# Two decode layers with a windowed KV cache: V pages issued from ScalarE's DMA queue instead of SyncE's

## The chip, the cores and the metric

The kernel runs on one core of one Trainium2 chip. The metric is the device time of one execution in microseconds (us). A core has the engines TensorE (PE in the profile, with PEld for its weight loads), VectorE (DVE), ScalarE (ACT), GpSimd (POOL) and SyncE (SP), and 16 DMA engines that move data between HBM and the on-chip memory. Each engine works through its own instructions in order. A DMA is started by an instruction of one of the engines, and stands in that engine's DMA queue; in this kernel these are SP's and ACT's.

## The reference

One token passes through attention and a gated feed-forward network (FFN), twice, with the same weights and caches both times. There are 32 heads of width 192, and each attends to the last 4096 positions of its own K and V cache.

```python
def _A_ref(x, k_cache, v_cache, wq, wo):      # x: (1, 1, 640); caches: (1, 32, 32768, 192), bf16
    W = min(4096, max(256, Sk // 4))          # 4096
    q = (x @ wq).reshape(B, Sq, Hq, Dh).transpose(0, 2, 1, 3)
    k = k_cache[:, :, Sk - W:, :]
    v = v_cache[:, :, Sk - W:, :]
    scores = jnp.einsum("bhqd,bhkd->bhqk", q, k) * (Dh ** -0.5)
    o = jnp.einsum("bhqk,bhkd->bhqd", _softmax(scores), v)
    return o.transpose(0, 2, 1, 3).reshape(B, Sq, Hq * Dh) @ wo

def _B_ref(x, w1, w3, w2):                    # 640 -> 1536 -> 640
    return (_silu(x @ w1) * (x @ w3)) @ w2

for _ in range(2):
    x = x + _A_ref(_layernorm(x), A_k_cache, A_v_cache, A_wq, A_wo)
    x = x + _B_ref(_layernorm(x), B_w1, B_w3, B_w2)
```

## The kernel before

All large data comes into one on-chip buffer, `arena`, of 16 slots of 128 x 6144 bf16 values (1.5 MB each; "page" below). A page is the K or the V window of one head, one fifth of wq, nine of the 48 chunks of wo, or a part of the FFN weights. The list `loads` (lines 147 to 172) fixes an order for all 145 of them. For each layer it holds the five q pages; then, step by step, the V page of head position i - 10 and the K page of position i; then six wo pages and four FFN pages (`fa` to `fd`). Text below numbers the loads 0 to 144 in this order: 0 to 4 are wq, 5 to 14 the first ten K pages, 15 the first V page, and from there V and K alternate. Loads 58 and 124 are the last K pages of the two layers, 68 and 134 the last V pages, 69 to 74 and 135 to 140 the wo pages, 75 to 78 and 141 to 144 the FFN pages. Some wo and FFN pages come in several DMAs.

`refill` (line 174) gives each free slot to the next load of the list and writes the DMA's issue, and `done` (line 186) frees a slot as its page has been used and calls `refill`. So an issue stands in the program just behind the last use of the page that held the slot. The K pages of 13 heads (`RETAIN`) stay in the arena from layer 0 to layer 1. In layer 0 they take slots away one by one, until three are left for all other loads: the last V pages, wo, the FFN, and wq of layer 1. In layer 1 each comes free with its use.

`attention` (line 407) runs over 42 steps. Step i multiplies the probabilities with V page i - 10 (`v_page`) and the query weights with K page i (`k_page`), whose 4-byte transposes on DVE come first (line 262). Eight heads are a block. After the last K page of a block, `softmax_head` takes maxima on DVE, writes one half of a bias on ACT (line 284) and the exponential on ACT (line 289). `build_w` then places the next block's query weights in `wst` (line 249 on ACT, line 251 on POOL), without which its K pages can't be multiplied. Two steps later, `softmax_place` copies the probabilities to `ptm` (line 302; five copies on ACT, three on DVE), without which the block's V pages can't. `combine` copies a finished block's sums on ACT (line 321). After the last step come `wo_proj`, the residual, a layer norm and `ffn`.

The helper `pin` keeps every engine's instructions in the order of the program text. Waits are set by the framework. A DMA waits for the last reader of its slot and for the slot's previous load. The framework also gives each DMA of SP and ACT one of eight completion counters, and a DMA waits until the previous transfer on its counter has landed. The counters are dealt out in the order in which the framework has scheduled the DMAs of both queues; with one queue, that is eight loads back.

Of the kernel before, what the change touches and what calls it, by code (L numbers as in the profile page):

```python
# [40 lines left out]
def kernel(  # L41
# [13 lines left out]
    nc = tc.nc  # L55
# [11 lines left out]
    def pin(ins):  # L67
        tc.keep_in_program_order(ins)
        return ins
# [104 lines left out]
    def refill():  # L174
        while free and loads:
            key, parts = loads.pop(0)
            s = free.pop(0)
            home[key] = s
            for off, n, src in parts:
                dst = arena[:, s * PGW + off:s * PGW + off + n] if off is not None else keep[:]  # L180
                pin(nc.sync.dma_start(out=dst, in_=src))  # L181

    def page(key):
        return arena[:, home[key] * PGW:home[key] * PGW + PGW]
# [1 line left out]
    def done(key):  # L186
        free.append(home.pop(key))
        refill()
# [218 lines left out]
    def attention(layer):  # L407
# [27 lines left out]
        wo_proj(layer)  # L435

    refill()
    ob = cst.tile([P, NCH], BF16, name="ob")
    for layer in range(2):
# [34 lines left out]
```

## Time and profile before

| what | value |
|---|---|
| time, median of 3 runs (lowest to highest) | 542.97 us (542.94 to 543.52) |
| span of the profiled execution, first to last instruction | 546.6 us |
| bytes moved, mean rate over the span | 224.34 MB, 410 GB/s |
| busy time of PE, DVE, ACT, POOL | 288.2, 222.9, 41.9, 13.2 us |
| packets on SP's queue (q1) and on ACT's (q10) | 22608 and 144 |
| rate from 0 to 14 us | 357 GB/s |
| rate from 306 to 318 us and from 318 to 330 us (between the layers) | 355 and 349 GB/s |
| rate from 530 to 541 us (last weights) | 301 GB/s |

The page splits the span into 40 slices and gives each engine's busy share by slice in tenths; the row "DMA" is the mean share of the 16 DMA engines. A row of instructions gives its start or its line, the time, engine, operation, and what it writes from what; brackets at its end hold the idle time of the engine before it and what ended that. In rows of DMA issues, "SPq" or "ACTq" is the queue of the issuing engine, and the last number is the median time from issue to landing. Rows of waits give the total, the count and the longest. A row for a stretch of time gives the busy time of PE, PEld, DVE, ACT and POOL, then PE's granted clock, the DMA share and GB/s. The rates of single stretches in the table are of this last kind.

### The profile page before, as it was taken

How to read it: one execution, taken by the hardware profiler on the slowest of the kernel's cores; microseconds unless marked ns; L12 is line 12 of the kernel's file. 1: busy time of each engine (PE TensorE's matmuls, PEld its weight loads, DVE VectorE, ACT ScalarE, POOL GpSimd, SP SyncE). 2: the span in 40 equal slices, each digit the busy share in tenths (PEclk: the TensorE clock that was granted, in tenths of full speed). 3: DMA queues.
4: the chain of work that ended last, by engine and by line, in shares of the span. 5: the costliest groups of instructions: out<-in, count | busy, mean ns of one | idle time of the engine just before them, and what ended most of it. 6: DMA issues, size and time to landing. Idle time of an engine off the chain costs nothing.

```text
span 546.6 us, 5673 instructions
## 1 busy us (share of the span) xinstructions
PE 288.2 (53%) x2400; PEld 119.9 (22%) x2400; DVE 222.9 (41%) x262; ACT 41.9 (8%) x107; POOL 13.2 (2%) x50
## 2 busy tenths in 40 slices
PE   2355455555564655743544356767465566553544
PEld 1111122222221222211222122333121222221211
DVE  2189755565446654410012057234524744530011
ACT  1100200020001100010001010211001100020000
POOL 5000000000000000000000000000000000000000
PEclk9579595667665776555556558896866766565656
DMA  8999999999999999999999989999999999999993
GB/s 353 430 420 428 421 427 424 424 423 424 426 424 423 424 427 422 423 418 428 417 389 397 370 355 419 424 426 422 425 421 426 423 427 427 423 425 423 420 415 156
DMA packets 22777, 224.34 MB, mean 410 GB/s; under 512 B 2784, under 2 KB 3168, under 8 KB 5472
## 3 DMA queue, kind: packets, MB, share of 16 engines
q1 hardware_dynamic: 22608, 223.98, 98.3%
q8 instruction: 19, 0.31, 0.2%
q14 instruction: 6, 0.05, 0.0%
q10 hardware_dynamic: 144, 0.00, 0.0%
HBM read 223.97 MB, written 0.00 MB: 410 GB/s over the span
## 4 chain that ended last, share of the span: by engine, by line
DMA 79%; PE 11%; DVE 6%; ACT 1%; issue 1%; SPq 1%; POOL 0%; ACTq 0%; DVEq 0%
DMA arena<-in_A_k_cache_dram 54%; DMA arena<-in_A_v_cache_dram 9%; DMA arena<-in_A_wo_dram 7%; PE s_ps L72 7%; DMA arena<-in_B_w_dram 5%; DVE arena L262 4%; DMA arena<-in_A_wq_dram 4%; PE o_ps L72 3%; PE y_ps L72 1%; SPq L181 1%; PE q_ps L72 1%; ACT w L289 0%; DVE t L274 0%; ACT ptm L302 0%; DVE w L292 0%
## 5 line engine op out<-in xcount | busy, mean ns | idle before, releaser
L72 PE MATMUL s_ps<-arena,wst 128*32 128x512 bf16 x768 | 164.0, 523 | 154.5 <-DVE arena L262 149.1
L262 DVE STREAM_TRANSPOSE arena<-arena 128x1536 uint32<-128x1536 uint32 x102 | 174.8, 1753 | 110.7 <-DMA arena<-in_A_k_cache_dram 108.8
L72 PE MATMUL o_ps<-arena,ptm 128*16 128x384 bf16 (+1 forms) x1024 | 129.3, 457 | 34.7 <-DMA arena<-in_A_v_cache_dram 33.6
L72 PEld LDWEIGHTS <-wst 128*32 128x32 bf16 x768 | 54.8, 115 | 248.5 <-issue 205.0
L72 PEld LDWEIGHTS <-ptm 128*16 128x16 bf16 (+1 forms) x1024 | 48.9, 106 | 76.5 <-issue 60.6
L325 DVE RECIPROCAL rl<-rl_ps 128x1 f32<-128x1 f32 x8 | 1.3, 168 | 62.0 <-PE rl_ps L72 62.0
L284 ACT ACTIVATE tb<-m 32x32 f32<-32x32 f32 x8 | 1.8, 228 | 307.4 <-DVE m L281 307.4
L72 PE MATMUL y_ps<-arena,otd 128*1 128x320 bf16 x192 | 16.8, 448 | 16.2 <-DMA arena<-in_A_wo_dram 16.2
L72 PE MATMUL q_ps<-arena,xs 128*32 128x384 bf16 x160 | 13.9, 500 | 20.3 <-DMA arena<-in_A_wq_dram 19.0
L274 DVE TENSOR_REDUCE t<-s_ps 64x1 f32<-64x512 f32 x8 | 5.5, 683 | 34.4 <-PE s_ps L72 34.4
L302 ACT COPY ptm<-w 32x128 bf16<-32x128 bf16 x40 | 16.2, 405 | 28.7 <-PE o_ps L72 26.4
L72 PEld LDWEIGHTS <-xs 128*32 128x32 bf16 x240 | 9.2, 123 | 40.2 <-issue 31.3
L209 DVE CAST w<-y_ps 128x320 bf16<-128x320 f32 x4 | 2.0, 491 | 37.8 <-PE y_ps L72 37.8
L251 POOL COPY wst<-qt_sb 32x48 bf16<-32x48 bf16 x16 | 6.2, 385 | 406.0 <-PE s_ps L72 236.8
L234 DVE CAST w<-q_ps 128x768 bf16<-128x768 f32 x2 | 1.9, 958 | 31.4 <-ACT w L232 31.4
L72 PEld LDWEIGHTS <-otd 128*1 128x1 bf16 x192 | 6.5, 101 | 26.5 <-issue 22.4
L292 DVE STREAM_TRANSPOSE w<-w 64x512 bf16<-64x512 bf16 x8 | 5.6, 704 | 7.2 <-ACT w L289 7.2
L321 ACT CAST w<-o_ps 128x384 bf16<-128x384 f32 x8 | 3.8, 478 | 52.1 <-PE o_ps L72 51.9
L72 PE MATMUL u_ps<-arena,xs 128*32 128x384 bf16 x40 | 4.2, 508 | 6.4 <-DMA arena<-in_B_w_dram 6.4
L72 PE MATMUL st_ps<-xsq,onesD 128*128 128x12 f32 x8 | 2.3, 367 | 9.2 <-DVE xsq L191 9.2
L375 DVE CAST w<-u_ps 128x384 bf16<-128x384 f32 x2 | 1.1, 558 | 14.6 <-PE u_ps L72 14.6
L249 ACT COPY wst<-qt_sb 32x48 bf16<-32x48 bf16 x16 | 6.4, 398 | 4.3 <-DVE qt_sb L242 4.0
(69 smaller groups left out, 86.7 us busy)
## 6 DMA issues: line engine op xcount, KB each, us to landing
arena<-in_A_v_cache_dram SPq DMA_DIRECT2D x64, 1536.0 KB, 29.5
arena<-in_A_k_cache_dram SPq DMA_DIRECT2D x51, 1536.0 KB, 29.5
arena<-in_A_wq_dram SPq DMA_DIRECT2D x10, 1536.0 KB, 10.9
arena<-in_A_wo_dram SPq DMA_DIRECT2D x6, 1440.0 KB, 15.6
arena<-in_B_w_dram SPq DMA_DIRECT2D x4, 1536.0 KB, 14.4
arena<-in_A_wo_dram SPq DMA_DIRECT2D x4, 960.0 KB, 16.9
arena<-in_A_wo_dram SPq DMA_DIRECT2D x6, 480.0 KB, 14.1
arena<-in_B_w_dram SPq DMA_DIRECT2D x2, 960.0 KB, 14.4
```

The lines of the kernel that those rows point to most:

```text
L72: return pin(nc.tensor.matmul(*a, **k))
L181: pin(nc.sync.dma_start(out=dst, in_=src))
L209: pin(nc.vector.tensor_copy(out=y_sb[:, 320:640], in_=y_ps[1][:, 0:320]))
L234: pin(nc.vector.tensor_copy(out=q_rep[par][:], in_=src))
L249: pin(nc.scalar.copy(out=dst, in_=src))
L251: pin(nc.gpsimd.tensor_copy(out=dst, in_=src))
L262: pin(nc.vector.transpose(x[:, w * sp:w * (sp + 1)].bitcast(U32), x[:, w * sp:w * (sp + 1)].bitcast(U32)))
L274: pin(nc.vector.reduce_max(out=t0[:, 0:1], in_=s_ps[0:64, :], axis=AX.X))
L284: pin(nc.scalar.mul(out=tb[32:64, :].rearrange("p (a z) -> p a z", a=4), in_=mb, mul=-SCALE))
L292: pin(nc.vector.transpose(et[:], e[:]))
L302: pin((eng.copy if eng is nc.scalar else eng.tensor_copy)(out=dst, in_=src))
L321: pin(nc.scalar.copy(out=o_sb[:, 0:384], in_=o_ps[:, 0:384]))
```

## The change

One line: DMAs of V pages are issued by ACT, all others by SP as before.

```diff
         for off, n, src in parts:
             dst = arena[:, s * PGW + off:s * PGW + off + n] if off is not None else keep[:]
-            pin(nc.sync.dma_start(out=dst, in_=src))
+            pin((nc.scalar if key[0] == "v" else nc.sync).dma_start(out=dst, in_=src))
```

The list of loads, the slots and the order of the instructions on PE, DVE and POOL stay as they were. SP keeps 51 K pages, ten wq pages and the pieces of wo and of the FFN. ACT's 64 V issues stand in its order where the loop writes them, between its copies and activations. Some of this order, from the built program, with the load whose landing each issue's counter asks for (another wait, for the slot, is left out):

```
layer 0, last K block: issue 59, 60, 61; bias and exponential of softmax 3; issue 62, 63; ptm copies; issue 64
layer 1, softmax 1:    issue 102 (95), 104 (97), 105 (99), 107 (101); bias and exponential; issue 109 (100);
                       wst copies; issue 111 (102); ptm copies; issue 113 (104)
layer 1, softmax 2:    issue 117 (109), 119 (111), 121 (113), 123 (115); bias and exponential; issue 125 (117);
                       wst copies; issue 126 (118), 127 (119), 128 (120); ptm copies; issue 129 (121)
layer 1, softmax 3:    issue 132 (125), 133 (128), 134 (130); bias and exponential; ptm copies
SP, end of layer 1:    eight pieces of wo, whose counters ask for loads 124, 126, 127, 129, 131, wo's first piece,
                       132, and wo's second piece
```

## The prediction

> **What bounds the kernel now.** I read the page's slices, queues and chain first, then the waits of SyncE's own queue, then stretches of the timeline where something other than the transfers might decide.
>
> ```profile
> span 546.6 us, 5673 instructions
> DMA  8999999999999999999999989999999999999993
> q1 hardware_dynamic: 22608, 223.98, 98.3%
> DMA 79%; PE 11%; DVE 6%; ACT 1%; issue 1%; SPq 1%; POOL 0%; ACTq 0%; DVEq 0%
> arena<-in_A_v_cache_dram SPq DMA_DIRECT2D x64, 1536.0 KB, 29.5
> arena<-in_A_k_cache_dram SPq DMA_DIRECT2D x51, 1536.0 KB, 29.5
> SPq L181 <- DMA arena<-in_A_v_cache_dram: 175.4, 57, 3.6
> 100.00:200.00 100.00, 56.04 (x398) 23.15 (x398) 53.80 (x55) 8.59 (x22) 1.53 (x4) 0.66 1.01 424
> ```
>
> One queue carries everything and fills the 16 DMA engines for 98.3% of the span: the share is 1.01 at 424 GB/s in the middle, PE is busy for 56 us of 100. So time can be lost only where the engines run dry, or where work behind the last transfer grows. A page takes 3.70 us and 29.5 us from issue to landing, so eight are in flight (29.5 / 3.70): each issue waits for the landing of the transfer eight before it on the same counter. That is the 175.4 us of waiting on SP, where nothing else queues.
>
> ```profile
> 0.75 2.57 SPq L181 DMA_DIRECT2D arena<-in_A_wq_dram  x5
> 14.31 0.83 PE L72 MATMUL q_ps<-arena,xs 128*32 128x384 bf16 x16 [2.09 <-DMA arena<-in_A_wq_dram]
> 18.00 1.47 PE L72 MATMUL q_ps<-arena,xs 128*32 128x384 bf16 x16 [2.86 <-DMA arena<-in_A_wq_dram]
> 222.97 3.44 DVE L262 STREAM_TRANSPOSE arena<-arena 128x1536 uint32<-128x1536 uint32 x2 [4.03 <-DMA arena<-in_A_k_cache_dram]
> 229.22 0.68 DVE L274 TENSOR_REDUCE t<-s_ps 64x1 f32<-64x512 f32 x1 [2.81 <-PE s_ps L72]
> 231.96 0.19 ACT L289 ACTIVATION_READ_ACCUMULATOR w<-s_ps,nbt 64x1 f32 x1
> 237.72 1.46 PE L72 MATMUL o_ps<-arena,ptm 128*16 128x384 bf16 x16 [0.84 <-DMA arena<-in_A_v_cache_dram]
> ```
>
> Pages 2 and 3 start PE at 14.31 and 18.00, so page 0 landed at 14.31 - 2 x 3.70 = 6.91; issued at 0.75, a page needs 6.2 us in an empty queue. At 222.97 the last K page of layer 0 (load 58) has landed; its scores are ready 6.3 us later and the exponential ends at 232.15, 9.2 us after the landing. Load 62 starts PE at 237.72.
>
> ```profile
> 509.02 1.46 PE L72 MATMUL o_ps<-arena,ptm 128*16 128x384 bf16 x16 [2.25 <-DMA arena<-in_A_v_cache_dram]
> 512.52 1.89 PE L72 MATMUL y_ps<-arena,otd 128*1 128x320 bf16 x24 [0.29 <-DMA arena<-in_A_wo_dram]
> 526.56 1.88 PE L72 MATMUL y_ps<-arena,otd 128*1 128x320 bf16 x24 [1.74 <-DMA arena<-in_A_wo_dram]
> 535.21 1.58 PE L72 MATMUL u_ps<-arena,xs 128*32 128x384 bf16 x16 [1.65 <-DMA arena<-in_B_w_dram]
> 541.03 0.72 PE L72 MATMUL y_ps<-arena,htd 128*1 128x320 bf16 x13 [0.77 <-DMA arena<-in_B_w_dram]
> ```
>
> The last V page (load 134) starts PE at 509.02; PE then waits for wo, for w3 and for w2.
>
> **The change, part by part.** Removed from SP: 64 issues of 0.33 us and their waits; SP has been waiting, not working, so this gives nothing. The cover is the eight pages in flight; without it each would cost 0.33 us, 21 us in all. Added to ACT: the same 64 issues, 21 us beside 41.9 us of work in 546.6. Their own time is hidden by the same cover; what matters is order and waits.
>
> First, two rings feed the same engines. I take it that each gets half while both hold work; no row shows it, since only the 1.2 KB of x runs on ACT's ring now. The bounds are that SP goes first (K lands as now), that pages alternate whole, and that their bytes mix, so that a K and a V page take 7.4 us together. At the start V page 24 (load 15) overtakes the q pages, and V pages follow as q and K pages are consumed. K pages come every 7.4 us and PE falls behind the landings by half the 16 slots, some 8 pages or 30 us. The engines don't notice: SP still holds about four K pages, because a slot is issued in the old order. Cost nothing; the cover is those pages, and if they were gone each miss would cost up to 6.2 us.
>
> Second, **the end of layer 0's K stream**, where 12 retained K pages leave four slots. Slots for loads 59, 60 and 61 come free when V loads 53, 55 and 57 are consumed, which is now before K 58 lands, and their V ring is its own: 59 alone (whole pages) or 59 and 60 (mixed) land ahead of K 58. Load 62 now stands on ACT behind the exponential of softmax 3, so it is issued 9.2 us after K 58's landing and lands 9.2 + 6.2 = 15.4 after. With one page ahead of K 58, two more pages (60, 61) and 62 itself would fill 3 x 3.70 = 11.1 us: 4.3 us of idle engines. With two ahead, 2 x 3.70 = 7.4: 8.0 us idle. With none, 14.8: 0.6. I take 6.1, midway between the two ways of sharing. What is late next is the wo, FFN and wq chain of the boundary, all SP's and bound by three slots as now: it moves as a block and returns nothing.
>
> Third, **layer 1**. Retained K pages let PE run ahead, so the V issues on ACT wait on counters, and softmax 1's exponential is queued behind loads 102, 104, 105 and 107, which wait for 95, 97, 99 and 101 to land. Counting from load 87 (landed 333.65), 99 and 101 are in after 13 pages: 333.65 + 13 x 3.70 = 381.8, where the exponential now runs at 365. The weight copies for the next K block stand behind load 109, that is behind the landing of 100, two pages on: 389. PE stalls some 20 us. At 389 loads 102 and 104 to 109 are issued and not landed: seven pages, 26 us of cover; the same count at softmax 2 (behind 117's landing) leaves 118 to 125 less one, again about seven. So I cost these stalls at nothing inside the layer; were the cover gone, each of the two would cost up to its 20 us.
>
> Fourth, **the tail**. Softmax 3 stands behind load 134's issue, which waits for 130 to land, and the wo pages are free on SP while loads 127 to 134 are still on ACT's ring. The counters hold wo back (its fifth piece waits for load 131, its seventh for 132), so between 3.8 pages (whole pages alternate: wo's first six pieces, 0.94 + 0.31 + 0.63 + 0.63 + 0.31 + 0.94) and all 5.0 land ahead of 134: 14.1 to 18.5 us later than 509.0. Of that PE's waits absorb: 134's matmuls and combine to 512.5, then 96 matmuls at 1.89 per 24, 7.6 us, would end at 520.1 where they end at 528.4, so 8.3, and 1.65 + 0.77 further on, 10.7 in all. The loss is 3.4 to 7.8; I take 5.6.
>
> Two rules of the Trainium skill bear on sharing. The row is 424 GB/s at a share of 1.01. "DMA: Bandwidth & Descriptors", section "Issuing engines are not separate DMA queues", says that issuing from several engines saves only sequencer time, since all use the same 16 engines; by it the gain is nothing, and the sum stands. Its section "Queues, rings and completion order" says that an engine drains a whole packet of one ring before it turns to the next, which would be the alternation of whole pages and a sum of 4.3 + 3.4; nothing in this trace has two busy rings.
>
> **Sum.** 6.1 + 5.6 = 11.7, against the span: 546.6 + 11.7 = 558.3. The span stands 3.6 above the median of the runs, 542.97, which gives 554.7. With whole pages 7.7 (550.7), with mixed bytes 15.8 (558.8).
>
> **The rivals.** (a) *Two rings move more.* Not slower: the engines overlap packets of two rings better. The best 4 us stretch of this trace ran at 437 GB/s, 3% above 424; over some 531 us of transfers (143.6 pages x 3.70) that is 16 us, less 11.7: 538.7. It decides from 2.2%, 433 GB/s. For it: stretches above 430 exist. Against: they neighbour slower ones, and eight pages in flight already give a share of 1.01. (b) *SP first, hidden anyway.* K keeps its places, the idle time is 0.6, and the tail has PE's 10.7 us of slack: 543.6. Against it: nothing ranks the rings, and the V ring is filled before the K pages that precede it are done. (c) *ACT's queue starves the engines.* A V issue blocked on a counter holds an exponential, PE stops, slots aren't freed, and the seven pages of cover run out. It decides when a stall exceeds 26 us; each of softmax 1 and 2 in layer 1 would then lose perhaps 5 us: 564.7. For it: the stalls are some 20 us, not far off; against: SP's K issues go on meanwhile.
>
> **How the numbers follow.** The forecast, slower by 8 to 16, has 0.62; (a) 0.14, of which about 0.03 ends within 0.2%; (b) 0.09, at 543.6 within 0.2% for 0.05 and slower for 0.04; (c) 0.15. What a measurement of this kernel can tell from no change is 0.2%, 1.1 us. So faster 0.11, same 0.08, slower 0.81. The forecast's own range is 550.7 to 558.8; from (b) to most of (c), with 0.1 left out at each end, it is 544 to 563.
>
> **What would show it.** Right: load 58 lands one or two pages (3.7 to 7.4 us) later than 222.9, a hole of 4 to 8 us in the DMA share follows, and no other hole is new; in layer 1 softmax 1 runs near 382 plus that shift while the share stays at 1.0; the last V page starts PE at 523 to 528 plus the shift, and at the end PE waits for no transfer. Wrong: GB/s in the middle off 424 by over 1%; K pages of the steady part landing 3.70 apart in pairs as now; holes near softmax 1 and 2 of layer 1; or the last matmuls still waiting for w2.

## The result, and the profile after

The changed kernel takes 549.75 us (median of 4 runs, 549.41 to 550.37), the kernel before 543.12 in the same session (542.94 to 543.52): a ratio of 1.0121, with a 95% interval of 1.0107 to 1.0134. It is 6.6 us slower; 554.7 was forecast, 11.7 us slower. The profiled execution of after is a run of 550.37 us with a span of 548.6; spans lie 1.7 to 1.8 us under the times. The profile of before that stands above has a span of 546.6, some 5 us more than its median of 543 implies. It was a long execution, and the first experiment below profiles that kernel again, in a run of 543.64 with a span of 541.9. Where the text below says "before", it reads that second profile.

First the page of after: the span, the DMA share and the rate by slice of 13.7 us, the two queues, and the chain.

```profile
span 548.6 us, 5688 instructions
DMA  8999999999999999979999999999999999999994
GB/s 351 426 424 424 426 424 423 425 424 424 424 425 425 423 426 422 393 288 427 392 395 405 424 412 410 419 428 424 421 428 421 425 428 422 424 423 420 424 417 167
q1 hardware_dynamic: 13392, 123.31, 54.1%
q10 hardware_dynamic: 9360, 100.67, 43.8%
DMA 75%; PE 14%; DVE 6%; ACT 2%; issue 1%; ACTq 0%; SPq 0%; POOL 0%; DVEq 0%
```

The V pages now run on q10, 43.8% of the span against 54.1% on q1; together 97.9%, where one queue had 98.3% in the first profile of before and 98.8% in the second. The rate away from the edges is 424 GB/s as before. One slice falls out: the 18th, 233 to 247 us, has 288 GB/s, and the one ahead of it 393. That is the end of layer 0's K stream. In stretches (the columns are busy time of PE, PEld, DVE, ACT and POOL, PE's granted clock, the DMA share and GB/s), after shows:

```profile
100.00:200.00 100.00, 53.00 (x401) 22.13 (x401) 57.39 (x57) 8.61 (x22) 1.54 (x4) 0.74 1.01 424
220.00:230.00 10.00, 4.70 (x29) 1.92 (x30) 5.38 (x4) 0.00 (x0) 0.00 (x0) 0.66 0.97 390
230.00:240.00 10.00, 5.59 (x56) 2.51 (x58) 4.78 (x12) 3.02 (x8) 0.00 (x0) 0.77 0.59 224
240.00:250.00 10.00, 4.57 (x44) 1.89 (x37) 1.09 (x3) 0.48 (x1) 0.00 (x0) 0.50 1.02 433
```

and before, in its second profile:

```profile
220.00:230.00 10.00, 6.49 (x53) 2.80 (x49) 4.16 (x4) 0.00 (x0) 0.00 (x0) 0.67 1.01 426
230.00:240.00 10.00, 5.14 (x55) 1.94 (x52) 3.64 (x13) 3.49 (x9) 0.00 (x0) 0.67 1.01 413
```

Over 220 to 250 us after moved (390 + 224 + 433) x 10 = 10,470 KB; at 424 GB/s that is 24.7 us of work in 30, so the engines stood idle for 5.3 us (before: 426, 413 and 426 GB/s, 0.2 us). The rows of after's timeline say which transfer was missing:

```profile
209.70 0.33 SPq L181 DMA_DIRECT2D arena<-in_A_k_cache_dram  x1
213.84 0.33 ACTq L181 DMA_DIRECT2D arena<-in_A_v_cache_dram  x1
218.93 0.34 ACTq L181 DMA_DIRECT2D arena<-in_A_v_cache_dram  x1
228.06 3.44 DVE L262 STREAM_TRANSPOSE arena<-arena 128x1536 uint32<-128x1536 uint32 x2 [4.03 <-DMA arena<-in_A_k_cache_dram]
234.00 0.68 DVE L274 TENSOR_REDUCE t<-s_ps 64x1 f32<-64x512 f32 x1 [2.51 <-PE s_ps L72]
236.16 0.68 ACT L289 ACTIVATE w<-s_ps,nbt 64x512 bf16<-64x512 f32 x1 [0.34 <-DVE nbt L286]
236.29 0.82 ACTq L181 DMA_DIRECT2D arena<-in_A_v_cache_dram  x2
242.76 1.46 PE L72 MATMUL o_ps<-arena,ptm 128*16 128x384 bf16 x16 [0.66 <-DMA arena<-in_A_v_cache_dram]
```

and the same two places before:

```profile
223.00 3.44 DVE L262 STREAM_TRANSPOSE arena<-arena 128x1536 uint32<-128x1536 uint32 x2 [4.03 <-DMA arena<-in_A_k_cache_dram]
237.74 1.46 PE L72 MATMUL o_ps<-arena,ptm 128*16 128x384 bf16 x16 [1.24 <-DMA arena<-in_A_v_cache_dram]
```

The last K page of layer 0 (load 58) starts its transposes at 228.06, where before they start at 223.00. The engines were full until then (418 GB/s in 226 to 228 us), so what it lacked went to other data: to loads 59 and 60, which ACT issued at 213.84 and 218.93, after SP had issued load 58 (209.70). The experiments below bear this out. The exponential of softmax 3 starts 8.1 us after the transposes, and only beside it does ACT issue loads 62 and 63 (236.29). Load 62 starts PE at 242.76; before, at 237.74. These 5.0 us are the hole.

### The profile page after: what moved, and what is told of

It is laid out like the page before. It is cut to its first block, busy times and chain, and to the rows that moved or that the text cites. A ratio compares the mean times of both kernels' runs of the same rounds, so it can differ in the third digit from the quotient of the medians.

```text
span 548.6 us, 5688 instructions
## 1 busy us (share of the span) xinstructions
PE 263.7 (48%) x2400; PEld 113.0 (21%) x2400; DVE 221.3 (40%) x262; ACT 41.9 (8%) x107; POOL 13.2 (2%) x50
## 3 DMA queue, kind: packets, MB, share of 16 engines
q1 hardware_dynamic: 13392, 123.31, 54.1%
q10 hardware_dynamic: 9360, 100.67, 43.8%
## 4 chain that ended last, share of the span: by engine, by line
DMA 75%; PE 14%; DVE 6%; ACT 2%; issue 1%; ACTq 0%; SPq 0%; POOL 0%; DVEq 0%
DMA arena<-in_A_v_cache_dram 33%; DMA arena<-in_A_k_cache_dram 31%; DMA arena<-in_A_wq_dram 7%; PE s_ps L72 7%; DVE arena L262 4%; PE y_ps L72 2%; PE o_ps L72 2%; DMA arena<-in_A_wo_dram 2%; DMA arena<-in_B_w_dram 2%; PE q_ps L72 1%; PE u_ps L72 1%; DVE t L274 0%; ACT ptm L302 0%; PE g_ps L72 0%; ACTq L181 0%
## 5 line engine op out<-in xcount | busy, mean ns | idle before, releaser
L72 PE MATMUL s_ps<-arena,wst 128*32 128x512 bf16 x768 | 153.1, 500 | 164.2 <-DVE arena L262 108.5
L72 PE MATMUL o_ps<-arena,ptm 128*16 128x384 bf16 (+1 forms) x1024 | 110.1, 421 | 54.3 <-DMA arena<-in_A_v_cache_dram 33.1
L72 PEld LDWEIGHTS <-wst 128*32 128x32 bf16 x768 | 52.9, 113 | 249.0 <-issue 213.5
L72 PEld LDWEIGHTS <-ptm 128*16 128x16 bf16 (+1 forms) x1024 | 42.4, 102 | 90.5 <-issue 55.2
L286 DVE STREAM_TRANSPOSE nbt<-tb 64x32 f32<-64x32 f32 x8 | 1.6, 203 | 47.5 <-ACT tb L284 47.1
L302 ACT COPY ptm<-w 32x128 bf16<-32x128 bf16 x40 | 16.2, 405 | 43.8 <-PE s_ps L72 27.0
L72 PE MATMUL y_ps<-arena,otd 128*1 128x320 bf16 x192 | 14.2, 441 | 5.9 <-DMA arena<-in_A_wo_dram 5.9
L72 PEld LDWEIGHTS <-otd 128*1 128x1 bf16 x192 | 6.2, 113 | 13.7 <-issue 8.6
L302 DVE COPY ptm<-w 32x128 bf16<-32x128 bf16 x24 | 6.3, 261 | 4.4 <-PE o_ps L72 3.6
L331 DVE SCALAR_TENSOR_TENSOR om<-ot_ps,rl,mask 128x192 bf16<-128x192 f32 x8 | 3.3, 418 | 8.4 <-PE ot_ps L72 8.2
## 6 DMA issues: line engine op xcount, KB each, us to landing
arena<-in_A_wo_dram SPq DMA_DIRECT2D x6, 1440.0 KB, 11.7
```

What stands on the lines that cost most here:

```text
L72: return pin(nc.tensor.matmul(*a, **k))
L302: pin((eng.copy if eng is nc.scalar else eng.tensor_copy)(out=dst, in_=src))
L331: pin(nc.vector.scalar_tensor_tensor(out=om[:], in0=ot_ps[:], scalar=rl[:], in1=mask[:].unsqueeze(2).broadcast_to([P, 16, 12]), op0=ALU.mu ...
```

## The experiments

All of them change only the condition by which `refill` chooses the issuing engine, so each computes the same thing. `key` is (kind, layer, head). In layer 0 the loads 59, 60 are heads 14, 15; loads 61 to 68 are heads 0 to 7. Each run stands against the kernel before on the same chip: 542.82 us (median of 23 runs) for layer 0 alone, layer 1 alone and loads 59 to 68; 542.72 (7 runs) for loads 64 to 68; 543.13 (23 runs) for the others. Losses in us are differences of medians. The ratios with their intervals are not quotients of these medians and differ from them by up to 0.1%: layer 0 alone loses 6.5 us by the medians and 6.1 (5.3 to 6.9) by its ratio. So differences of some tenths between losses say little.

### The kernel before once more

No edit.

> The kernel before once more, for a second profile. The spans of the changed kernel's four executions lie 1.7 to 1.8 us under their times; the first profile of the kernel before has a span 3.6 us above the median of its runs, so that execution was some 5 us longer than usual. Theory: this one has a span near 541.3 and a rate above 400 GB/s between 306 and 330 us, where the first showed 355 and 349. Rival: the boundary between the layers always loses there, and the span is again near 546.

Its time is 543.64, its span 541.9. At 306 to 318 and 318 to 330 us it shows 424 and 390 GB/s, where the profile above has 355 and 349. So the loss between the layers is that one execution's. The two profiles agree within 0.2 us up to wo's last piece (278.20 for 278.03), and part from there: the fifth wq page starts PE at 313.28 in the second and 317.15 in the first, the last V page at 503.73 and 509.02. So nothing behind 280 us must be compared with the first profile.

### Layer 0 alone, and layer 1 alone

```diff
-pin(nc.sync.dma_start(out=dst, in_=src))
+pin((nc.scalar if key[0] == "v" and key[1] == 0 else nc.sync).dma_start(out=dst, in_=src))   # layer 0 only
+pin((nc.scalar if key[0] == "v" and key[1] == 1 else nc.sync).dma_start(out=dst, in_=src))   # layer 1 only
```

> V pages of layer 0 on ACT, those of layer 1 on SP as before. Theory (K's last page of layer 0 comes late, its engines then run dry; the tail of layer 1 costs the rest): the hole of 5.0 us alone, 543.1 + 5.0 = 548.1, between 547.3 and 549. Rival (what costs is ACT's issues holding back the softmax of layer 1): 543.1 to 543.8.

> V pages of layer 1 on ACT, those of layer 0 on SP as before. Theory: only the tail, which is the rest of 6.6 us, 1.6: 544.7, between 543.8 and 545.5; softmax 1 and 2 are still some 20 us late and the DMA share stays at 1.0 beside them. Rival: 548 to 550, with holes in the DMA share near softmax 1 or 2.

Layer 0 alone takes 549.33 us (548.60 to 550.27): 1.0112 (1.0098 to 1.0127), 6.5 us over before. Layer 1 alone takes 542.72 (542.33 to 544.47): 1.0002 (0.9993 to 1.0011). Both lie outside what was expected, and in opposite directions: layer 0 carries the whole loss and a little more than the hole, and layer 1 with its tail costs nothing. A row of layer 0 alone:

```profile
230.00:240.00 10.00, 6.12 (x52) 2.54 (x51) 4.83 (x12) 2.88 (x8) 0.00 (x0) 0.66 0.55 203
```

The hole is there as in after. Counted from the second profile of before, load 62 starts PE 5.15 us late, load 67 5.13, wo's last piece 6.31 (284.51 for 278.20), the fifth wq page 6.49 (319.77 for 313.28). So 1.2 to 1.4 us more come between load 67 and layer 1. How the tail of layer 1 alone went is shown further down.

### Which of the V pages do it

Layer 0's V pages stay on ACT's queue but for some at the end, which go back to SP's:

```diff
+... key[0] == "v" and key[1] == 0 and not (key[2] < 8 or key[2] in (14, 15)) ...   # loads 59 to 68 on SP
+... key[0] == "v" and key[1] == 0 and key[2] not in (14, 15) ...                   # loads 59, 60 on SP
+... key[0] == "v" and key[1] == 0 and key[2] not in (1, 2) ...                     # loads 62, 63 on SP
```

> V pages of layer 0 on ACT, save the last ten (loads 59 to 68), which are back on SP; layer 1 on SP. Loads 59 and 60 now stand behind load 58 in one ring. Theory (they overtook it): the K page lands as in the kernel before, no hole, 543.1 to 543.9. Rival (PE, some 30 us behind the landings through layer 0, is what runs the engines dry at the end): the hole stays for the larger part, 546 to 548.

> As the run with layer 0's V pages on ACT, but loads 59 and 60 issued from SP, behind load 58 in its ring. Theory: load 58 lands near 223 and the hole of 5.1 us goes, also with load 62 behind the exponential: 549.3 - 5.1 = 544.2, between 543.4 and 545. Rival (PE's lag or ACT's order makes the hole): 547 or more.

> As the run with layer 0's V pages on ACT (549.3 there), but loads 62 and 63 issued from SP, where nothing stands before them but load 58: 62 no longer stands behind the exponential of softmax 3. Theory (loads 59 and 60 overtake load 58 in the other ring; ACT's order is a small part): 62 is issued at the end of load 59's use, some 1.7 us earlier, 547.6, between 546.8 and 548.5. Rival (ACT's order makes the hole): the hole goes, 543.5 to 545.

| on SP's queue | time (lowest to highest) | ratio (95%) | GB/s in 230 to 240 us |
|---|---|---|---|
| none (layer 0 alone, above) | 549.33 (548.60 to 550.27) | 1.0112 (1.0098 to 1.0127) | 203 |
| loads 59 to 68 | 543.17 (542.51 to 543.53) | 1.0004 (0.9996 to 1.0013) | 421 |
| loads 59 and 60 | 544.13 (543.46 to 547.52) | 1.0021 (1.0006 to 1.0036) | 407 |
| loads 62 and 63 | 548.11 (547.18 to 548.32) | 1.0083 (1.0067 to 1.0099) | 292 |

With loads 59 and 60 behind load 58 in one queue, load 58 is on time, and the hole is gone. The transposes of load 58, and then the stretch, with loads 59 and 60 on SP:

```profile
222.86 3.44 DVE L262 STREAM_TRANSPOSE arena<-arena 128x1536 uint32<-128x1536 uint32 x2 [0.33 <-DMA arena<-in_A_k_cache_dram]
```

```profile
230.00:240.00 10.00, 5.50 (x52) 1.93 (x52) 2.57 (x7) 3.27 (x8) 0.00 (x0) 0.55 1.02 407
```

Moving these two pages back takes the loss from 6.5 us (549.33 less 542.82) to 1.0 (544.13 less 543.13; by the ratio 0.3 to 2.0). Where the 1.0 arises isn't shown: in the profiled execution the fifth wq page starts PE at 313.15, before at 313.28. Taking loads 62 and 63 out of ACT's order instead lets load 62 be issued at 234.59 rather than 236.64 (layer 0 alone), and gains some 1.5 us (the loss is 5.0, 548.11 less 543.13): ACT's order is the smaller part, the overtaking the larger. With 59 to 68 on SP nothing is lost, though the other 22 V pages of layer 0 run on ACT's queue.

Then the whole change but for these ten pages:

```diff
+... key[0] == "v" and not (key[1] == 0 and (key[2] < 8 or key[2] in (14, 15))) ...
```

> The changed kernel (V pages of both layers on ACT) save loads 59 to 68, which go back to SP. Theory: the whole loss of the change lies at those ten loads, so 542.5 to 543.5, the same as before, though PE falls behind in both layers and softmax 1 and 2 of layer 1 are late. Rival (the two layers' delays add to something): 544 or more.

543.12 us (542.34 to 546.18), 0.9998 (0.9985 to 1.0012). Ten of the 64 pages make the whole loss; the other 54 are neither gain nor loss.

### The last 1.2 to 1.4 us

The theory was that they come of load 68 and the wo pieces taking turns in two rings. It was tried twice, with load 68 on SP, and with 64 to 68:

```diff
+... key[0] == "v" and key[1] == 0 and key[2] != 7 ...            # load 68 on SP
+... key[0] == "v" and key[1] == 0 and not 3 <= key[2] < 8 ...    # loads 64 to 68 on SP
```

> As the run with layer 0's V pages on ACT, but load 68, the last V page of layer 0, issued from SP, ahead of wo's first piece in one ring. In that run load 67 starts PE 5.1 us later than in the kernel before, 68 8.3 us later and wo's last piece 6.3 us later. Theory: wo's first pieces overtake 68 in the three slots of the boundary and cost 1.2 us after the hole: 548.1, between 547.4 and 548.8. Rival (the 1.2 us have another cause): 549.3.

> As the run with layer 0's V pages on ACT (549.3, 6.5 above the kernel before of its call), but loads 64 to 68 issued from SP, so that the last V pages and wo stand in one ring as before; loads 59 to 63 stay on ACT, and with them the hole. What is open: at load 66 that run is 5.1 us late, at the fifth wq page of layer 1 6.5. Theory: the 1.4 us come of two rings taking turns where three slots are left, so 5.1 above the kernel before, between 4.5 and 5.7. Rival: they come of the hole itself, through what it does to the chain behind it, and stay: 6.2 or more.

Load 68 on SP: 549.62 us (548.71 to 549.91), 1.0109 (1.0092 to 1.0126). Loads 64 to 68 on SP: 548.94 (548.58 to 550.02), 1.0119 (1.0103 to 1.0136). The theory falls: in both the loss stays at 6.2 to 6.5 us. In the second, load 68 starts PE 4.91 us late (264.84 for 259.93), and the fifth wq page 5.59 (318.87 for 313.28), with 0.8 of the difference arising between load 68 and wo's first piece; the span of that execution is only 5.0 over before's, while the median is 6.2 over. The rival in the last expectation, that the rest comes of the hole itself and stays at 6.2 or more, fits the 6.2. So does the run with loads 59 and 60 on SP: load 68 starts PE 2.1 us late there too (262.06 for 259.93), but there is no hole, and the fifth wq page is on time. As far as these profiles show, then, the rest comes with the hole; by what step isn't settled. No kernel here is faster than before.

## Why the prediction was right, point by point

*What bounds the kernel.* Right. 424 GB/s at a share of 1.01 in 100 to 200 us before (the row in the prediction) and after. With it goes rival (a), that two rings move more, which needed 433. The 64 issues on ACT and those gone from SP cost and give nothing: 54 pages on ACT's queue, 0.9998.

*First, the shares of the two rings.* Between the two ways offered, the bytes mix. The K pages of the steady part of after (transposes on DVE, each of which waited for its page):

```profile
45.38 3.44 DVE L262 STREAM_TRANSPOSE arena<-arena 128x1536 uint32<-128x1536 uint32 x2 [1.57 <-DMA arena<-in_A_k_cache_dram]
51.39 3.44 DVE L262 STREAM_TRANSPOSE arena<-arena 128x1536 uint32<-128x1536 uint32 x2 [2.57 <-DMA arena<-in_A_k_cache_dram]
58.79 3.44 DVE L262 STREAM_TRANSPOSE arena<-arena 128x1536 uint32<-128x1536 uint32 x2 [3.96 <-DMA arena<-in_A_k_cache_dram]
63.86 3.44 DVE L262 STREAM_TRANSPOSE arena<-arena 128x1536 uint32<-128x1536 uint32 x2 [1.64 <-DMA arena<-in_A_k_cache_dram]
```

They are 6.01, 7.40 and 5.07 us apart: not multiples of the 3.70 us of a page, as whole pages in turn would give. The prediction had read a rule of the Trainium skill so ("DMA: Bandwidth & Descriptors", section "Queues, rings and completion order": an engine drains a whole packet of one ring before it turns to the next), taking the page for the packet. The queue rows speak against that: q10 went from 144 packets to 9360 with 64 V pages, so a page is 144 packets. If these are the rule's packets, which no run here shows, turns by packets mix two pages, and the rule agrees with the spacings. Its use in the prediction, whole pages in turn, doesn't, though the midpoint taken there hid it.

*Second, the end of layer 0's K stream.* Right in place, cause and size. Load 58 came 5.1 us late (3.7 to 7.4 expected), load 62 was issued 8.2 us after it (9.2), and the engines were idle for 5.3 us (4.3 to 8.0; 6.1 taken). The experiments separate the cause: with loads 59 and 60 behind load 58 the hole is gone; with 62 and 63 out of ACT's order some 1.5 us of it are. One detail was off: load 61 was to be free before load 58 landed, but was issued at 228.14, just behind it, so the rate fell from there on (252 GB/s in 228 to 230 us). What failed is its last sentence, that the boundary "moves as a block and returns nothing". In layer 0 alone it moved by 5.1 us at load 67 and by 6.5 at the fifth wq page. This is 1.2 to 1.4 us more; they come with the hole, and the step that makes them is open.

*Third, layer 1's softmaxes.* Right, at no cost. Rows of ACT in after, with those of DVE and PE that waited for it:

```profile
358.80 27.02 ACTq L181 DMA_DIRECT2D arena<-in_A_v_cache_dram  x7
385.92 0.23 ACT L284 ACTIVATE tb<-m 32x32 f32<-32x32 f32 x1 [28.12 <-DMA arena<-in_A_k_cache_dram]
386.18 0.20 DVE L286 STREAM_TRANSPOSE nbt<-tb 64x32 f32<-64x32 f32 x1 [14.15 <-ACT tb L284]
390.84 0.82 ACT L249 COPY wst<-qt_sb 32x48 bf16<-32x48 bf16 x2 [3.58 <-DMA arena<-in_A_v_cache_dram]
391.76 1.89 PE L72 MATMUL s_ps<-arena,wst 128*32 128x512 bf16 x8 [20.88 <-ACT wst L249]
450.01 0.23 ACT L284 ACTIVATE tb<-m 32x32 f32<-32x32 f32 x1 [43.90 <-DMA arena<-in_A_v_cache_dram]
450.27 0.20 DVE L286 STREAM_TRANSPOSE nbt<-tb 64x32 f32<-64x32 f32 x1 [25.98 <-ACT tb L284]
458.31 1.89 PE L72 MATMUL s_ps<-arena,wst 128*32 128x512 bf16 x8 [29.45 <-ACT wst L249]
501.11 0.23 ACT L284 ACTIVATE tb<-m 32x32 f32<-32x32 f32 x1 [31.41 <-DMA arena<-in_A_v_cache_dram]
```

Seven issues are spread over 27 us, and the three softmaxes stand behind such issues. ACT was idle for 28, 44 and 31 us before them, but that isn't all delay, since for part of it their maxima weren't ready: DVE, which needs ACT's half of the bias, was held for 14.15 and 25.98 us at softmax 1 and 2 and for 6.82 at softmax 3. Softmax 1 runs at 385.92 and the weight copies at 390.84. Expected were 382 and 389 plus the shift, which against the first profile, whose times the forecast used, is 2.6 us at the fifth wq page (319.80 for 317.15). A stretch of after with softmax 1, for all engines:

```profile
345.00:400.00 55.00, 27.00 (x267) 11.82 (x266) 14.10 (x27) 7.01 (x19) 1.54 (x4) 0.69 1.01 424
```

The share stays at 1.01, and around softmax 2 it is 1.00 to 1.02 (425, 423 and 429 GB/s from 430 to 460 us). So the cover held, and rival (c) is out. But the count behind it was too low: PE stalled for 20.9 and 29.5 us, where some 20 were expected each time, and the second is longer than the 26 us of seven pages at which rival (c) was to begin. At 3.70 us a page, eight pages came in during it. In layer 1 alone the stretch at softmax 1 has 424 GB/s, its stalls are 22.48 and 29.45 us, and that kernel costs 0.

*Fourth, the tail: the step that failed.* The loss was put at 3.4 to 7.8 us, 5.6 taken; layer 1 alone measured -0.1 us (542.72 against 542.82). Its PE rows at the end:

```profile
517.33 1.46 PE L72 MATMUL o_ps<-arena,ptm 128*16 128x384 bf16 x16 [5.70 <-DMA arena<-in_A_v_cache_dram]
520.33 4.21 PE L72 MATMUL y_ps<-arena,otd 128*1 128x320 bf16 x96
530.15 1.57 PE L72 MATMUL u_ps<-arena,xs 128*32 128x384 bf16 x16 [0.67 <-DMA arena<-in_B_w_dram]
536.02 0.97 PE L72 MATMUL y_ps<-arena,htd 128*1 128x320 bf16 x11 [0.80 <-DMA arena<-in_B_w_dram]
```

and those of before, second profile:

```profile
503.73 1.46 PE L72 MATMUL o_ps<-arena,ptm 128*16 128x384 bf16 x16 [2.24 <-DMA arena<-in_A_v_cache_dram]
507.24 1.88 PE L72 MATMUL y_ps<-arena,otd 128*1 128x320 bf16 x24 [0.29 <-DMA arena<-in_A_wo_dram]
...
521.28 1.89 PE L72 MATMUL y_ps<-arena,otd 128*1 128x320 bf16 x24 [1.73 <-DMA arena<-in_A_wo_dram]
529.90 1.58 PE L72 MATMUL u_ps<-arena,xs 128*32 128x384 bf16 x16 [1.61 <-DMA arena<-in_B_w_dram]
...
535.76 0.85 PE L72 MATMUL y_ps<-arena,htd 128*1 128x320 bf16 x11 [0.79 <-DMA arena<-in_B_w_dram]
```

The mechanism is there. The wo pieces overtook the V pages, and the last V page came 13.6 us late (517.33 less 503.73; 14.1 to 18.5 expected). What was mis-sized is the work behind it: the 96 wo matmuls, put at 7.6 us as four times a group of 24 in 1.89, took 4.21 in one go. So they ended at 524.54, 1.4 us after before's 523.17, and the wait for w3, 1.61 us before and 0.67 now, took most of that; w2 is waited for as ever. By the prediction's own sum the lower end, 3.4, loses 3.4 (7.6 less 4.2) and 0.5 (14.1 less 13.6), which leaves nothing. Two things kept the group's duration from carrying over. A group by itself takes longer than its share of a long run at the same clock: in after, where most of the 96 ran at a granted clock of 0.50 as before, they took 5.62 us, 1.4 per 24. And the clock rises. Layer 1 alone, the y matmuls only (PE, DVE, ACT busy, clock, share, GB/s):

```profile
522.00:524.00 2.00, 2.00 (x68) 0.00 (x0) 0.00 (x0) 1.00 1.02 430
```

and after, in the same work:

```profile
528.00:530.00 2.00, 2.00 (x40) 0.00 (x0) 0.00 (x0) 0.50 1.07 450
532.00:534.00 2.00, 1.47 (x40) 0.35 (x1) 0.40 (x1) 0.92 0.95 383
```

68 matmuls ran in 2 us at a granted clock of 1.00, 40 at 0.50. Before, each group waits for its piece, and the mean clock over 500 to 530 us is 0.50. That a PE which works without pauses is granted the full clock after some microseconds is what the Trainium skill, "TensorE: Matmul & The Clock Gate", section "The HAM clock gate (the 'warmup' mystery)", says; the run of 96 without a wait agrees with it. The time it took differs: the clock rose at some 522 in layer 1 alone, 5 us after the last V page started PE (517.33), and at some 532 in after, 7 us after (524.85). In after the end of the kernel lies at most 0.4 us behind that of layer 0 alone (medians of 549.75 and 549.33; each against its own kernel before, 6.6 and 6.5 us): PE waits for no transfer there, as forecast, so its slack was used up, but not exceeded by much.

```profile
524.85 1.46 PE L72 MATMUL o_ps<-arena,ptm 128*16 128x384 bf16 x16 [5.71 <-DMA arena<-in_A_v_cache_dram]
527.85 5.62 PE L72 MATMUL y_ps<-arena,otd 128*1 128x320 bf16 x96
542.69 0.86 PE L72 MATMUL y_ps<-arena,htd 128*1 128x320 bf16 x19 [0.86 <-DVE htd L390]
```

*The sum.* 6.1 + 5.6 = 11.7 forecast. Measured: 5.1 for the hole, 1.2 to 1.4 behind it, which no term held, 0 to 0.4 for the tail, 6.6 in all. So the direction came of the hole alone, and the closeness of 6.1 to the 6.5 that layer 0 loses is in part luck. The time missed the forecast's own range (550.7 to 558.8) by 1 us at the low end and lies in the wide one. Also, the sum was made on a span that was itself 5 us too long; taking it back to the median kept that out of the forecast. Rival (b), K first and the tail hidden, was right about the tail and wrong about load 58.

## What to carry to other kernels

Where the DMA engines are full, as here, a second queue added no bandwidth, but it gave up the order between the two streams. While many buffers were free this cost nothing; where few are left (three or four here), a page that is needed later lands ahead of the one that frees the next buffer, and the engines run dry: look there first, and keep those few transfers in one queue. When you price work that is now to run behind a late transfer, don't take the duration it has between waits, where TensorE ran at half clock here: 96 matmuls without pauses took 4.21 us, where four groups of 24 would make 7.6.

## What the runs showed of the hardware

- Softmaxes held up for 14 and 26 us behind ACT's DMA issues, and PE stalls of 21 and 29 us behind them, cost nothing while transfers already issued, or issued meanwhile, kept the share at 1.00 to 1.02.
- ACT started a DMA issue at 236.29 while its exponential (236.16 to 236.84) was still running; the activation that stands ahead of the issue didn't hold it to its end. Layer 0 alone shows the same (issue at 236.64, exponential from 236.52 for 0.68 us).
- One execution of the kernel before lost some 4 us between the layers (the fifth wq page at 317.15 for 313.28), at 349 to 355 GB/s (306 to 330 us) and a DMA share of 0.89 to 0.94; another one ran that stretch at 390 to 424. Why isn't known. It isn't where layer 0 alone loses its unexplained time: of those 1.4 us, 1.2 arise between load 67 and wo's last piece, by 285 us.
